# The first x block in two loads, the order of the first products, and fewer warming products, in a float32 kernel of one core

## The chip, the cores and the metric

The kernel runs on 1 core of one Trainium2 chip. The metric is the device time of one execution in microseconds (us); where several executions are shown, their median. A profile comes from one execution, and its own time is given beside it.

## The reference

x is 2048 x 512 (float32). The result mixes two branches with a gate that depends on the row:

```python
g = sigmoid((x * gate_w).sum(-1, keepdims=True))
a = dft_seq_re @ (x @ dft_hid_re.T) - dft_seq_im @ (x @ dft_hid_im.T)   # 2048x2048 and 512x512
b = (silu(x @ w1) * (x @ w3)) @ w2                                      # w1, w3: 512x1376, w2: 1376x512
out = g * a + (1 - g) * b
```

## The kernel before, in words

Products are made in float32 precision out of float32r operands: each operand is split into a rounded part (`high`, a copy on ScalarE, line 108) and the remainder (`low`, a subtraction on VectorE, line 111), and a product of two blocks is three matmuls: rounded x rounded, rounded x remainder, remainder x rounded. Below they are hh, hl and lh, with the weight's part first in the tuple of the code. A block product is done by Strassen's method in Winograd's form (seven products of half blocks instead of eight), so most operands are sums of blocks that VectorE makes.

The kernel writes out its order by hand (`tc.manual_schedule()`, line 427): the order of the calls is the order of each engine's instructions, and each engine and each DMA queue works in that order.

Stages, in order:

1. **The start** (lines 427 to 537). The loads go to SyncE's queue: the first quarter of weight block 0 (`load_w(0, 0, 1)`, 128 x 256), the x block B11 (`load_xo(0, "B11")`, 128 x 1024), the other three quarters of weight block 0, the x blocks B21, B12 and B22, then weight blocks 1 to 3. While they come, TensorE runs `WARM` = 11 products of constants in bfloat16 (lines 432 and 433), whose result nobody reads. The very first column block (weights 0) is not done by Strassen's method but by eight plain half products, `half(i, j, w, x, start)` (line 447): weights' form w (`None` for a21) times x form x (`None` for b12) into the bank C[i, j]. One `half` is six matmuls: two row tiles r of the contraction with hh, hl and lh each. Row tile r reads the x half r (512 columns of the loaded block), so the first row tile needs only the first half of the block. The first call, `half(0, 0, 0, 0, True)` (line 485), reads weights quarter 0 and B11; the second, `half(1, 0, None, 0, True)` (line 487), reads a21 (the fourth quarter of the weights) and B11; the third and fourth (lines 493 and 495) read the second and third quarter and B21; the fifth and sixth (lines 498, 502) read B12.
2. **Gate and up products** (the loop at line 744, `gate_up`), one step for each column block of w1 and w3 and each half of x, with Strassen's seven products.
3. **The spectral branch, the down projection and the hidden DFT** (lines 880 to 1053): `step(m)` for eight blocks of 28 steps or fewer each, one step being 12 matmuls of 512 columns or more. Four blocks of kind F, then two H, then two Y. Six "late" operands (`late_load`, `late_sums` and so on, lines 813 to 844) are loaded, summed, split and stored during the F blocks, hidden beside the products; `late_load` issues its load on SyncE's queue.

The lines that set the order of the first products are these:

```python
hh, lh, hl = (0, 0), (1, 0), (0, 1)
order = [(r, *p) for r in range(2) for p in ((hh, hl, lh) if w is None else (hh, lh, hl))]
if w == x == 0:
    order = [(r, *p) for some in ((hh, lh), (hl,)) for r in range(2) for p in some]
```

`split_by_both` (line 477) rounds a half block with two engines: ScalarE the first 256 columns, VectorE (a copy, line 480) the other 256, and VectorE then makes the remainder.

Of the kernel before, what the change touches and what calls it, by code (L numbers as in the profile page):

```python
# [21 lines left out]
NG = NST // 2  # L22
NC = (F + P - 1) // P
NP2 = (NC + 1) // 2
WARM = 11
LOOK = 3
K = 9
W2_AT = (9, 11, 13, 15)
# [4 lines left out]
def fnet_swiglu_gate_kernel(  # L33
# [20 lines left out]
    nc = tc.nc  # L54
# [25 lines left out]
    def bank(k, name):  # L80
        return psum.tile([P, 512], F32, tag=f"ps{k}", name=name)
# [8 lines left out]
    def take(places, shape, dtype, name):  # L90
        p, tag = at = places.pop(0)
        t = p.tile(shape, dtype, tag=tag, name=name)
        HELD[id(t)] = t, places, at
        return t

    def wide(name):
        return take(F4, [P, 1024], F32, name)
# [9 lines left out]
    def high(hi, src):  # L107
        nc.scalar.activation(hi, src, AF.Copy)  # L108

    def low(hi, lo, src):  # L110
        nc.vector.tensor_sub(lo, src, hi.bitcast(F32))  # L111

    def split(hi, lo, src):
        high(hi, src)
        low(hi, lo, src)
# [5 lines left out]
    def matmul(ps, u, v, some=slice(None), **kw):  # L121
        nc.tensor.matmul(ps.rearrange("p (n a) -> p n a", a=2), u, turns(v)[:, some], **kw)  # L122
# [18 lines left out]
    def flat(ap):  # L141
        return ap.rearrange("p a n -> p (a n)")
# [55 lines left out]
    XO, ST = {}, {}  # L198
    XRAW = ("B12", "B11", "B21", "B22")
# [9 lines left out]
            XO[2] = xo1.tile([P, 2, 2, 512], F32R, tag="xo6", name="xo1_6")  # L209
        return XO[2]  # L210

    def load_xo(g, k):

        if g not in XO:
            XO[g] = (xo1 if g else xo0).tile([P, 2, 7 - g, 2, 512], F32R, tag="xo", name=f"xo{g}")
        ST[g, k] = wide(f"xs{g}_{k}")
        nc.sync.dma_start(ST[g, k], xt[g, XRAW.index(k)])

    OPS = ("B11", "B21", "B22", "T1", "T2", "T3", "T4")
    SUMS = {"T1": ("B12", "B11"), "T2": ("B22", "T1"), "T3": ("B22", "B12"), "T4": ("B21", "T2")}  # L220
# [17 lines left out]
    def load_w(w, lo=0, hi=4):  # L238
        if lo == 0:
            WS[w] = f4_a.tile([P, 4, 256], F32, tag=f"f4_{4 + w % (LOOK + 1)}", name=f"ws{w}")  # L240
        nc.sync.dma_start(WS[w][:, lo:hi].rearrange("p a n -> p (a n)"),  # L241
                          w13[SETS[w], :, lo * 256 : hi * 256])
# [7 lines left out]
    def wa_parts(w, lo, hi):  # L250
        return (*(flat(WA[w][:, h, lo:hi]) for h in range(2)), flat(WS[w][:, lo:hi]))

    def new_wa(w):

        WA[w] = wap.tile([P, 2, 3, 256], F32R, tag="wa", name=f"wa{w}")
# [169 lines left out]


    ctx.enter_context(tc.manual_schedule())
    load_w(0, 0, 1)
    load_xo(0, "B11")
    warm = nc.const_aps.tensor(1.0, [P, 512], mybir.dt.bfloat16)  # L430
    wps = bank(7, "wps")
    for n in range(WARM):
        nc.tensor.matmul(wps, warm[:, :P], warm, start=True, stop=True)
    nc.scalar.activation(act0, warm[:, :24], AF.Silu)
    load_w(0, 1, 4)
    for k in ("B21", "B12", "B22"):
        load_xo(0, k)
    load_w(1)
    load_w(2)
# [7 lines left out]
    def half(i, j, w, x, start):  # L447

        wp = lambda h, sl: a21[:, h, sl] if w is None else WA[0][:, h, w, sl]
        xp = lambda q, h: b12[:, h, q * 512 : (q + 1) * 512] if x is None else XO[0][:, h, x, q, :]
        hh, lh, hl = (0, 0), (1, 0), (0, 1)
        order = [(r, *p) for r in range(2) for p in ((hh, hl, lh) if w is None else (hh, lh, hl))]
        if w == x == 0:
            order = [(r, *p) for some in ((hh, lh), (hl,)) for r in range(2) for p in some]
        for n, (r, u, v) in enumerate(order):
            matmul(C[i, j], wp(u, slice(r * P, (r + 1) * P)), xp(r, v),
                   start=start and n == 0, stop=not start and n == 5)

    def xo_half(k, q):
        i = OPS.index(k)
        return XO[0][:, 0, i, q], XO[0][:, 1, i, q], ST[0, k][:, q * 512 : (q + 1) * 512]
# [8 lines left out]

    t1 = hp.tile([P, 1024], F32, tag="h", name="t1")
    new_wa(0)
    split(*wa_parts(0, 0, 1))

    def split_by_both(hi, lo, src):

        high(hi[:, :256], src[:, :256])
        nc.vector.tensor_copy(hi[:, 256:], src[:, 256:])  # L480
        low(hi, lo, src)

    split_by_both(*xo_half("B11", 0))
    split(*xo_half("B11", 1))
    half(0, 0, 0, 0, True)
    split(a21[:, 0], a21[:, 1], WS[0][:, 3])
    half(1, 0, None, 0, True)
    high(*wa_parts(0, 1, 3)[::2])
    low(*wa_parts(0, 1, 2))
    split_by_both(*xo_half("B21", 0))  # L490
    split(*xo_half("B21", 1))
    low(*wa_parts(0, 2, 3))
    half(0, 0, 1, 1, False)
    split(b12[:, 0], b12[:, 1], ST[0, "B12"])
    half(1, 0, 2, 1, False)
# [63 lines left out]
    for k in ("B11", "B21", "B12", "B22"):  # L559
        do(at_end, 1, load_xo, 1, k)  # L560
# [60 lines left out]
    for n in range(NI):  # L621
        if n in W2_AT:
            p = W2_AT.index(n)
# [4 lines left out]
        if n in A1_AT:  # L628
            p = A1_AT.index(n)
# [183 lines left out]
    def late_load(i, src, tag):  # L813

        r, m = (flat(ut.tile([P, 2, 512], F32, tag=k, name=f"{k}p{i}")) for k in (tag, "c21"))
        nc.sync.dma_start(r, src)
        LATE[i] = [r, m]

    def late_pair(i, j):
# [207 lines left out]
    for i, (src, sp, p) in enumerate(late):  # L1027
        blk, b = 1 + i // 3, i % 3
        n = (10, 17, 24)[b]
        at(blk, n - (5, 5, 6)[b], late_load, i, src[p], ("u3", "u3", "u2")[b])  # L1030
        at(blk, n, late_sums, i)
        at(blk, n + 1, late_split1, i)
        at(blk, n + 2, late_split2, i)
        for j in range(2):
            at(blk, n + 2 + j, late_store, i, j, sp[j][p])
            at(blk, n + 4 + j, late_free, i, j)
# [82 lines left out]
```

## Time and profile before

| | |
|---|---|
| median of 3 runs | 675.94 us (675.76 to 676.01) |
| the profiled execution, its own time | 675.5 us |
| span from its first to its last instruction | 673.7 us |
| mean granted TensorE clock | 1.000 |
| data moved | 172.54 MB, 256 GB/s on average |

The span is the time between the first and the last instruction that the profiler recorded; the chip's own time holds a little more. Engines are PE (TensorE; PEld is its weight loads, which run beside the matmuls), DVE (VectorE), ACT (ScalarE), POOL (GpSimd) and SP (SyncE, which here only issues loads and stores; SPq is its queue). Names such as `xs_B<-xt` are a destination and a source: `xs_B` is a loaded x block, `ws` a loaded weight block, `wa` and `a` split weights, `xo` split x, `C` the banks of the first products, `X`, `Y`, `Z` those of the gate products, `P` those of the last stage. A matmul's recorded length includes the pipeline's end, so its pace is read from the starts.

### The profile page before, as it was taken

To read this page: it belongs to the slowest core of one execution; us is meant where nothing else is said; L and a number is where in the kernel's file an instruction comes from. 1 tells how busy PE (TensorE), PEld (TensorE's weight loads), DVE (VectorE), ACT (ScalarE), POOL (GpSimd) and SP (SyncE) were. 2 spreads that over 40 slices of the span, in tenths; PEclk is the share of its full clock that TensorE was granted. 3 is DMA by queue.
4 is the path that set the end of the run, shared out by engine and by line. 5 is a ranking of instruction groups with operands and counts; after the bars stand their busy time and mean duration, and the time that the engine had idled before them with its cause. 6 is when DMAs were issued, how large, how long until landed. Compare 5 with 4: busy or idle time off the path is not lost.

```text
span 673.7 us, 8669 instructions
## 1 busy us (share of the span) xinstructions
PE 669.4 (99%) x3101; PEld 583.1 (87%) x3101; DVE 601.6 (89%) x748; ACT 371.9 (55%) x496; POOL 64.5 (10%) x119
## 2 busy tenths in 40 slices
PE   9999999999999999999999999999999999999998
PEld 6888888888888888888888888888888888888887
DVE  6999988887779999978999899978896897898996
ACT  6765666655547764465554654554445455455451
POOL 0012112221110000001110101100000000000000
PEclk9999999999999999999999999999999999999999
DMA  7576657599998676715696279919996772874942
GB/s 280 208 293 249 229 200 266 194 357 356 423 418 317 224 216 223 293 63 205 229 386 242 90 252 349 367 57 348 391 341 235 286 259 86 312 277 157 338 134 93
DMA packets 45563, 172.54 MB, mean 256 GB/s; under 512 B 5328, under 2 KB 5712, under 8 KB 41680
## 3 DMA queue, kind: packets, MB, share of 16 engines
q1 hardware_dynamic: 32480, 118.11, 49.0%
q0 software_dynamic: 12752, 53.49, 20.1%
q8 instruction: 24, 0.39, 0.2%
q10 hardware_dynamic: 288, 0.39, 0.2%
q14 instruction: 19, 0.16, 0.1%
HBM read 114.82 MB, written 57.16 MB: 255 GB/s over the span
## 4 chain that ended last, share of the span: by engine, by line
PE 98%; DMA 1%; ACT 0%; DVE 0%; SPq 0%; issue 0%
PE P L122 68%; PE X L122 16%; PE Z L122 8%; PE Y L122 4%; PE C L122 2%; DMA xs_B<-xt 1%; DMA out<-zc 0%; DVE zc L869 0%; ACT xo L108 0%; SPq L241 0%; ACT zc L876 0%
## 5 line engine op out<-in xcount | busy, mean ns | idle before, releaser
L122 PE MATMUL P<-zo,a 128*128 128x512 f32 x1344 | 290.4, 379 | 0.0
L108 ACT ACTIVATE zo<-B 128x1024 fp32r<-128x1024 f32 (+1 forms) x182 | 188.3, 1041 | 176.1 <-PE P L122 79.4
L122 PEld LDWEIGHTS P<-zo,a 128*128 128x128 f32 x1344 | 253.8, 189 | 36.4 <-DVE zo L111 0.4
L111 DVE TENSOR_TENSOR zo<-B,zo 128x1024 fp32r<-128x1024 f32 (+1 forms) x182 | 217.7, 1203 | 29.4 <-ACT zo L108 28.9
L122 PE MATMUL P<-zo,H 128*128 128x512 f32 x468 | 101.2, 379 | 0.0
L122 PEld LDWEIGHTS P<-zo,H 128*128 128x128 f32 x468 | 88.5, 189 | 12.6
L711 DVE TENSOR_TENSOR B<-B,B 128x1024 f32<-128x1024 f32 (+1 forms) x78 | 93.0, 1192 | 0.1
L122 PE MATMUL X<-xo,wb 128*128 128x512 f32 x378 | 88.6, 379 | 0.0
L122 PEld LDWEIGHTS X<-xo,wb 128*128 128x128 f32 x378 | 71.4, 189 | 10.2
L122 PE MATMUL P<-zo,Y 128*128 128x512 f32 (+1 forms) x336 | 71.6, 375 | 0.0
L122 PEld LDWEIGHTS P<-zo,Y 128*128 128x128 f32 x336 | 62.7, 189 | 8.7
L714 DVE TENSOR_TENSOR B<-B,B 128x1024 f32<-128x1024 f32 x26 | 31.7, 1220 | 0.0
L347 POOL DMA_DIRECT2D hsp<-h x40 | 21.7, 544 | 101.4 <-DVE h L407 70.9
L122 PE MATMUL X<-xo,wa 128*128 128x512 f32 x126 | 30.6, 379 | 0.0
L122 PE MATMUL Y<-xo,wa 128*128 128x512 f32 x126 | 30.6, 379 | 0.0
L122 PE MATMUL Z<-xo,wb 128*128 128x512 f32 x126 | 30.6, 379 | 0.0
L122 PE MATMUL Z<-xo,wa 128*128 128x512 f32 x126 | 30.6, 379 | 0.0
L122 PEld LDWEIGHTS X<-xo,wa 128*128 128x128 f32 x126 | 23.8, 189 | 3.4
L122 PEld LDWEIGHTS Y<-xo,wa 128*128 128x128 f32 x126 | 23.8, 189 | 3.4
L122 PEld LDWEIGHTS Z<-xo,wb 128*128 128x128 f32 x126 | 23.8, 189 | 3.4
L122 PEld LDWEIGHTS Z<-xo,wa 128*128 128x128 f32 x126 | 23.8, 189 | 3.4
L967 ACT ACTIVATE zu<-P 128x512 f32<-128x512 f32 x30 | 17.7, 596 | 15.1 <-PE P L122 12.7
(147 smaller groups left out, 552.8 us busy)
## 6 DMA issues: line engine op xcount, KB each, us to landing
B<-cc SPq DMA_DIRECT2D x64, 512.0 KB, 5.8
hsp<-h POOLq DMA_DIRECT2D x40, 256.0 KB, 4.1
B<-hsp SPq DMA_DIRECT2D x20, 512.0 KB, 5.5
wbsp<-wb POOLq DMA_DIRECT2D x8, 1024.0 KB, 4.3
wb<-wbsp SPq DMA_DIRECT2D x8, 1024.0 KB, 7.6
B<-zsp SPq DMA_DIRECT2D x16, 512.0 KB, 8.5
H<-w2sp SPq DMA_DIRECT2D x6, 1024.0 KB, 9.5
ws<-w SPq DMA_DIRECT2D x11, 512.0 KB, 5.0
```

The lines of the kernel that those rows point to most:

```text
L108: nc.scalar.activation(hi, src, AF.Copy)
L111: nc.vector.tensor_sub(lo, src, hi.bitcast(F32))
L122: nc.tensor.matmul(ps.rearrange("p (n a) -> p n a", a=2), u, turns(v)[:, some], **kw)
L347: nc.gpsimd.dma_start(hsp[g, b + k, j // 2, :, j % 2 * 512 : (j % 2 + 1) * 512], h)
L711: nc.vector.tensor_add(t, t, RAW[blk, b, q][:, :n])
L714: nc.vector.tensor_sub(t, RAW[blk, "B12", q], t)
L967: nc.scalar.activation(U[name][:, r], ps[r], AF.Copy)
```

## The change

B11 comes in two loads of 128 x 512, its first half ahead of the first weights' quarter, its second behind it; B21 comes in two loads as well. Eight warming products instead of eleven. B11's first half is rounded by VectorE alone (one copy of 512 columns) and ahead of the weights; its remainder is made before that of the weights. The first `half` goes row tile by row tile: hh, hl, lh for the first, hh, lh, hl for the second. The fifth `half` (weights 0 times b12) does hh and lh of both row tiles and then both hl. The fourth (third quarter times B21) does hl ahead of lh. The third quarter of the weights is rounded behind the first half of B21 instead of together with the second quarter. Of the late loads, those with i = 0 and 3 are issued by GpSimd's queue.

```diff
-WARM = 11
+WARM = 8
...
-    def load_xo(g, k):
+    def load_xo(g, k, some=(0, 2)):
...
-        ST[g, k] = wide(f"xs{g}_{k}")
-        nc.sync.dma_start(ST[g, k], xt[g, XRAW.index(k)])
+        if some[0] == 0:
+            ST[g, k] = wide(f"xs{g}_{k}")
+        b = slice(some[0] * 512, some[1] * 512)
+        nc.sync.dma_start(ST[g, k][:, b], xt[g, XRAW.index(k), :, b])
...
+    load_xo(0, "B11", (0, 1))
     load_w(0, 0, 1)
-    load_xo(0, "B11")
+    load_xo(0, "B11", (1, 2))
...
     load_w(0, 1, 4)
-    for k in ("B21", "B12", "B22"):
+    for q in range(2):
+        load_xo(0, "B21", (q, q + 1))
+    for k in ("B12", "B22"):
         load_xo(0, k)
...
-        order = [(r, *p) for r in range(2) for p in ((hh, hl, lh) if w is None else (hh, lh, hl))]
+        order = [(r, *p) for r in range(2)
+                 for p in ((hh, lh, hl) if w == 1 or w and x == 2 else (hh, hl, lh))]
         if w == x == 0:
+            order[3:] = [(1, *p) for p in (hh, lh, hl)]
+        if w == 0 and x is None:
             order = [(r, *p) for some in ((hh, lh), (hl,)) for r in range(2) for p in some]
...
+    nc.vector.tensor_copy(*xo_half("B11", 0)[::2])
+    low(*xo_half("B11", 0))
     split(*wa_parts(0, 0, 1))
...
-    split_by_both(*xo_half("B11", 0))
     split(*xo_half("B11", 1))
     half(0, 0, 0, 0, True)
     split(a21[:, 0], a21[:, 1], WS[0][:, 3])
     half(1, 0, None, 0, True)
-    high(*wa_parts(0, 1, 3)[::2])
-    low(*wa_parts(0, 1, 2))
+    split(*wa_parts(0, 1, 2))
     split_by_both(*xo_half("B21", 0))
+    high(*wa_parts(0, 2, 3)[::2])
     split(*xo_half("B21", 1))
     low(*wa_parts(0, 2, 3))
     half(0, 0, 1, 1, False)
...
-        nc.sync.dma_start(r, src)
+        (nc.gpsimd if i in (0, 3) else nc.sync).dma_start(r, src)
```

## The prediction

> **What bounds the kernel now.** I read the page's head and its busy shares first, to see whether any engine has idle time to give back.
>
> ```profile
> span 673.7 us, 8669 instructions
> PE 669.4 (99%) x3101; PEld 583.1 (87%) x3101; DVE 601.6 (89%) x748; ACT 371.9 (55%) x496; POOL 64.5 (10%) x119
> ```
>
> TensorE is busy for 99% of the span. The chain that ended last, in order of time, says where the rest lies (start, length, what):
>
> ```profile
> 1.18 3.75 DMA xs_B<-xt
> 5.42 10.88 PE C L122 x48
> ...
> 206.66 461.18 PE P L122 x2136
> 668.58 1.97 DMA out<-zc
> ```
>
> The chain is one load, then TensorE from 5.42 to 668.58 without a break, then the last store. Its main piece runs at 461.18 / 2136 = 0.216 us a product, and that is the full pace: nothing there can be shortened by a load or a split, only by fewer products, and the change keeps the products. So all that this change can win lies ahead of the point from which the products run at 0.216 without a gap. The timeline of the first 17 us finds that point (start, length, engine, line, what, and in brackets the idle time ahead and its releaser).
>
> ```profile
> 0.74 0.39 SPq L241 DMA_DIRECT2D ws<-w  x1
> 0.78 4.33 PE L433 MATMUL wps<-const-bfloat16-1.0 128*128 128x512 bf16 x11 [0.78 <-PEq L1108]
> 1.18 0.42 SPq L217 DMA_DIRECT2D xs_B<-xt  x1
> 1.65 0.42 SPq L241 DMA_DIRECT2D ws<-w  x1
> 2.12 1.48 SPq L217 DMA_DIRECT2D xs_B<-xt  x3
> 3.15 0.42 ACT L108 ACTIVATE wa<-ws 128x256 fp32r<-128x256 f32 x1 [0.89 <-DMA ws<-w]
> 4.96 0.94 ACT L108 ACTIVATE xo<-xs_B 128x256 fp32r<-128x256 f32 x2 [1.39 <-DMA xs_B<-xt]
> 4.96 0.29 DVE L480 CAST xo<-xs_B 128x256 fp32r<-128x256 f32 x1 [0.94 <-DMA xs_B<-xt]
> 5.40 1.29 DVE L111 TENSOR_TENSOR xo<-xs_B,xo 128x512 fp32r<-128x512 f32 x2 [0.15 <-ACT xo L108]
> 5.42 1.81 PE L122 MATMUL C<-xo,wa 128*128 128x512 f32 x6 [0.31 <-ACT xo L108]
> 6.18 0.42 ACT L108 ACTIVATE a<-ws 128x256 fp32r<-128x256 f32 x1 [0.29 <-DMA ws<-w]
> 6.50 0.61 ACT L108 ACTIVATE wa<-ws 128x512 fp32r<-128x512 f32 x1
> 6.63 0.43 DVE L111 TENSOR_TENSOR a<-ws,a 128x256 fp32r<-128x256 f32 x1
> 6.75 0.19 PEld L122 LDWEIGHTS C<-xo,wa 128*128 128x128 f32 x1 [0.29 <-DVE xo L111]
> 7.07 1.46 PE L122 MATMUL C<-xo,a 128*128 128x512 f32 x6
> 7.48 0.94 ACT L108 ACTIVATE xo<-xs_B 128x256 fp32r<-128x256 f32 x2 [0.36 <-DMA xs_B<-xt]
> 8.37 2.75 PE L122 MATMUL C<-xo,wa 128*128 128x512 f32 x12
> 8.72 1.06 ACT L108 ACTIVATE b<-xs_B 128x1024 fp32r<-128x1024 f32 x1 [0.31 <-DMA xs_B<-xt]
> 9.81 1.23 DVE L111 TENSOR_TENSOR b<-xs_B,b 128x1024 fp32r<-128x1024 f32 x1 [0.26 <-ACT b L108]
> 14.61 1.82 DVE L111 TENSOR_TENSOR wa<-ws,wa 128x768 fp32r<-128x768 f32 x2
> 16.14 1.46 PE L122 MATMUL X<-xo,wa 128*128 128x512 f32 x6
> ```
>
> Six products at 0.216 are 1.30 us. The second group, at 7.07, hands over at 8.37, exactly 1.30 later, and the third and fourth (x12) are twice that. The first, at 5.42, takes 1.65. So 0.35 us of gaps lie inside the first group, and the gap-free run begins with the second, at 7.07. Whatever starts earlier must move the third group's start, 8.37, or it moves nothing. The chip's time of this execution is 675.5 us, the span 673.7, so 1.8 us lie around it; the median of the runs shown is 675.94, or 0.44 above this execution. I work in the span and carry the difference over to the median.
>
> **The change part by part: the loads.** One queue carries them. The 131 kB quarter of the weights, issued at 0.74, set ScalarE to work at 3.15; the 524 kB x block behind it did so at 4.96. By then 655 kB had come. In the new order the half block (262 kB) is first, the quarter second, and the other half third, so the 655 kB are complete as before, at 4.96. For the first two I interpolate by bytes between 3.15 and 4.96: half a block at 3.15 + 131/524 x 1.81 = 3.60, the quarter at 4.06. Bounds: not before 3.15, where a load of half the size stood, and not after 4.96.
>
> The weights' other three quarters (393 kB) woke ScalarE at 6.18, the next x block at 7.48, the next at 8.72. That is 1.30 and 1.24 us for 524 kB each. The two extra loads cost SyncE two more issues of some 0.45 us, which put the remaining weights' issue at about 2.1 instead of 1.65, still 4 us ahead of their landing. I take 6.18 and 8.72 as unchanged, and put the first half of B21 at 6.18 + 1.30/2 = 6.83. What each extra load costs beyond its bytes the trace doesn't separate: the bounds are 0 and 0.45 (its issue laid end to end), and I take 0, because the loads already stand back to back in the queue.
>
> The Trainium skill, "DMA: Bandwidth & Descriptors", section "Anatomy of one DMA", gives a fixed 2.0 us per load beside its bytes. Paid one after the other, that would be an estimate of 4 us for the two extra loads, some 679 in all; the wakes 1.30 and 1.24 us apart show that loads in one queue don't pay it one after the other, so it gets no chance below.
>
> **The first group.** Three finer rows give single durations:
>
> ```profile
> 5.28 0.61 ACT L108 ACTIVATE xo<-xs_B 128x512 fp32r<-128x512 f32 x1
> 6.01 0.69 DVE L111 TENSOR_TENSOR xo<-xs_B,xo 128x512 fp32r<-128x512 f32 x1
> 6.75 0.48 PE L122 MATMUL C<-xo,wa 128*128 128x512 f32 x1
> ```
>
> VectorE now copies the whole half. The row has 0.29 for 256 columns; 512 lie between 0.29 and 0.58, and I take 0.42: the 128x256 and 128x512 subtractions (0.43, 0.69) share a fixed part of some 0.16, and 0.29 is that plus 0.13. Copy 3.60 to 4.02, its remainder 4.05 to 4.74, the weights' remainder from 4.66 (two subtractions started 0.61 apart at 5.40 and 6.01) to 5.08. ScalarE rounds the weights from 4.06 to 4.48 (0.42), so the first product is at 4.52, 0.90 earlier. But row tile 1 waits for the second half: rounded by ScalarE 4.96 to 5.57, its remainder 5.60 to 6.29. The new order puts that remainder last, so the sixth product is at 6.33; before, it was at 6.75.
>
> **The second group**, half(1, 0), wants the weights a21. They land at 6.18 as before and are rounded by 6.60, so it starts at 6.64, and this is what ends last. A product that waited takes 0.32 to the next (6.75 to 7.07); the third wants the remainder of a21 (6.64 + 0.43 = 7.07) and waits some 0.03. Six products: 6.64 + 0.32 + 0.22 + 0.25 + 3 x 0.216 = 8.08. **The third group therefore starts at 8.08 instead of 8.37: a gain of 0.29 us**, of the 0.90 by which the first product moved.
>
> **Behind it.** ScalarE rounds wa's second piece from 6.50 to 6.92 (started 0.32 behind a21, as now) and the first 256 columns of B21 by 7.34. VectorE, laid end to end: remainder of a21 to 7.07, of wa's piece to 7.49, the copy of the other 256 columns to 7.78, remainder of B21's first half to 8.50, of its second, 0.61 behind, to 9.11. Group three wants the copy at 8.08, the first remainder with its third product at 8.51 and the second with its sixth at 9.16: it just fits, and each 0.1 us that VectorE is later costs as much. B12 lands at 8.72 and has its remainder at 11.04 (9.81 + 1.23). Group five would start at 10.67; in its old order it would want that remainder at 11.10, in the new one (both remainders last) at 11.53, so that reorder secures the gain and costs nothing. Does VectorE follow?
>
> ```profile
> 8.00:16.00 8.00, 8.00 (x39) 6.93 (x38) 7.68 (x9) 6.35 (x9) 0.00 (x0) 1.00 0.77 313
> 16.00:24.00 8.00, 8.00 (x39) 7.01 (x38) 7.97 (x12) 7.41 (x12) 0.69 (x1) 1.00 0.23 68
> ```
>
> Columns behind the length are busy us of each engine (PE, PEld, DVE, ACT, POOL): VectorE has 7.68 and 7.97 of 8, so it can't move forward by itself. The products have to fit ahead of its results as they stand. The first gate group (16.14, then 15.85) wants the remainder of its weights with its third product, at 16.28; that is done at 14.61 + half of 1.82 = 15.52. The cover is 0.76, above the 0.29.
>
> **The warming products** fall from 11 to 8.
>
> ```profile
> 3.72 0.15 PEld L433 LDWEIGHTS <-const-bfloat16-1.0 128*128 128x128 bf16 x1 [0.28 <-issue]
> 4.14 0.15 PEld L433 LDWEIGHTS <-const-bfloat16-1.0 128*128 128x128 bf16 x1 [0.28 <-issue]
> 4.51 0.10 PEld L433 LDWEIGHTS <-const-bfloat16-1.0 128*128 128x128 bf16 x1 [0.22 <-issue]
> ```
>
> They step by 0.42 to 0.43 and the step shrinks (0.37, and a load of 0.10 for 0.15) between 4.14 and 4.51: TensorE speeds up there. Eight of them stream until about 4.14, so TensorE idles from 4.14 to 4.52. The eleven would have ended at 5.11 and held the first product back by 0.59, but not the second group, which waits for a21; the reduction itself is worth nothing at 8.08. Its price if the speed-up fails to come is the first rival.
>
> **The late loads** with i = 0 and 3 (two of six) move to GpSimd's queue.
>
> ```profile
> 281.26 0.54 POOL L785 DMA_DIRECT2D p5g<-gs  x1 [0.17 <-issue]
> 356.24 0.54 POOL L859 DMA_DIRECT2D zsp<-zc  x1 [2.93 <-DVE zc L857]
> 304.77 0.42 DVE L150 TENSOR_TENSOR c21p<-u3p 128x256 f32<-128x256 f32 x1
> 377.41 0.42 DVE L150 TENSOR_TENSOR c21p<-u3p 128x256 f32<-128x256 f32 x1
> DMA to landing us min/median/max: 4.4/5.8/7.7
> ```
>
> Behind those stores they would be issued at about 281.8 and 356.8 and land within 7.7, at 289.5 and 364.5; the sums that read them start at 304.77 and 377.41. With 13 us of cover I cost them at nothing; behind them on GpSimd wait only stores, which nothing in this stage reads. Without that cover the price would be the delay itself.
>
> **The rivals.** *The speed-up is late* (slower). It came 3.36 to 3.73 us after the first matmul at 0.78. If the idle 0.38 us before 4.52 restarts that count, it comes at 7.9 to 8.25. Until then products step by 0.43: nine have started by 7.96, three more follow at 0.22 or so, and the third group starts near 8.9: 0.5 later than before, 676.4. It decides from the point where the idle stretch is long enough not to count as work. Against it: eight matmuls already fill 3.36 us and the gap is 0.38 long. A second lost period of 3.4 us would add half of it, 1.7: 678.1.
>
> The Trainium skill, "TensorE: Matmul & The Clock Gate", Part 1, says that the full clock follows one busy window of about 3.4 us, in a free-running frame. Eight warming products are just about that long and would seldom fill such a window, which speaks for this rival; the trace's release after 3.36 to 3.73 us agrees with the length, and no trace here shows how much idle a window forgives.
>
> *The gain is lost on the way.* If the smaller loads land 0.3 us later (a21 at 6.48 and B21 behind it; the two unseparated issues would make it at most 0.9), the second group starts at 6.94 and the third near 8.4, or VectorE is that much late for B21's remainders: 675.9. For: each wake hangs on one queue. Against: 1.24 to 1.30 us per 524 kB is steady.
>
> *a21 lands earlier.* Then the second half's remainder (6.33) ends last: 0.31 more at best, 675.3.
>
> **How the numbers follow.** Forecast 0.62: 675.94 - 0.29 = 675.65, rounded to 675.6. Lost on the way 0.17, 675.9. Speed-up late by one period 0.13, 676.4; by two 0.04, 678.1. Earlier a21 0.04, 675.3. The runs shown lie 0.25 apart. The range 675.1 to 676.5 reaches from the last case less that scatter to the first rival and a little beyond. A measurement of this kernel can tell about 0.2%, 1.35 us, from no change, and all cases but the double loss lie within it: same 0.94, slower 0.05, faster 0.01, since 1.35 is more than the first group's gaps and even the whole 0.90 of the earlier first product would give.
>
> **What would show it.** ScalarE's or VectorE's first x work near 3.6 and the first product near 4.5: the loads are right. Second group at 6.6 behind a21, third at 8.1: the sum is right. Products stepping 0.43 beyond 4.6 show the first rival; a21's rounding later than 6.3 shows the second. A gap in TensorE after 9 us, or VectorE waiting for the late loads, would prove me wrong.

## The result, and the profile after

The changed kernel takes 678.0 us (median of 18 runs, 676.25 to 680.41) beside 675.96 for the kernel before (18 runs, 675.68 to 677.98). The ratio is 1.0031, 95% interval 1.0021 to 1.0040: slower by some 2.1 us, and spread over 4.2 us. The profiled execution took 679.74, its span is 678.0.

The chain that ended last in the kernel after (start, length, what), for comparison with 5.42, 206.66 and 461.18 before:

```profile
1.66 5.11 DMA xs_B<-xt
7.47 12.74 PE C L122 x45
...
210.85 461.15 PE P L122 x2136
```

The long stage of products has kept its length, 461.15; it begins 4.19 us later in this execution. So the loss is ahead of it, where the gain was sought. The timeline of the kernel after, its start:

```profile
0.78 3.57 PE L436 MATMUL wps<-const-bfloat16-1.0 128*128 128x512 bf16 x8 [0.78 <-PEq L1117]
4.13 0.43 DVE L483 CAST xo<-xs_B 128x512 fp32r<-128x512 f32 x1 [4.13 <-DMA xs_B<-xt]
4.43 0.42 ACT L108 ACTIVATE wa<-ws 128x256 fp32r<-128x256 f32 x1 [2.18 <-DMA ws<-w]
4.90 1.66 PE L122 MATMUL C<-xo,wa 128*128 128x512 f32 x3 [0.55 <-ACT wa L108]
6.79 0.63 ACT L108 ACTIVATE xo<-xs_B 128x512 fp32r<-128x512 f32 x1 [1.94 <-DMA xs_B<-xt]
7.47 1.65 PE L122 MATMUL C<-xo,wa 128*128 128x512 f32 x3 [0.91 <-ACT xo L108]
7.74 0.42 ACT L108 ACTIVATE a<-ws 128x256 fp32r<-128x256 f32 x1 [0.33 <-DMA ws<-w]
8.91 2.77 PE L122 MATMUL C<-xo,a 128*128 128x512 f32 x6
10.38 1.06 ACT L108 ACTIVATE b<-xs_B 128x1024 fp32r<-128x1024 f32 x1 [0.66 <-DMA xs_B<-xt]
11.47 3.56 PE L122 MATMUL C<-xo,wa 128*128 128x512 f32 x12
14.87 1.46 PE L122 MATMUL C<-b,wa 128*128 128x512 f32 x6
```

Two things are seen. **The data are late**: the second half of B11 is rounded at 6.79 (the whole block: 4.96), a21 at 7.74 (6.18), B12 at 10.38 (8.72), always behind the DMA. **The products are slow**: the second group goes from 8.91 to 11.47, 2.56 us for six where it took 1.30.

The first is plain in the windows' last columns, DMA share and GB/s. Kernel after, then kernel before:

```profile
3.00:4.00 1.00, 1.00 (x4) 0.16 (x2) 0.00 (x0) 0.00 (x0) 0.00 (x0) 1.00 0.75 201
4.00:5.00 1.00, 0.45 (x2) 0.10 (x1) 0.83 (x2) 0.42 (x1) 0.00 (x0) 1.00 1.07 265
5.00:6.00 1.00, 1.00 (x3) 0.76 (x3) 0.62 (x2) 0.00 (x0) 0.00 (x0) 1.00 0.80 221
6.00:7.00 1.00, 0.56 (x2) 0.00 (x0) 0.00 (x0) 0.21 (x1) 0.00 (x0) 1.00 0.79 215
7.00:8.00 1.00, 0.53 (x1) 0.50 (x2) 0.55 (x1) 0.68 (x2) 0.00 (x0) 1.00 1.02 394
```

```profile
3.00:4.00 1.00, 1.00 (x4) 0.31 (x3) 0.41 (x1) 0.42 (x1) 0.00 (x0) 1.00 1.00 375
4.00:5.00 1.00, 1.00 (x4) 0.25 (x2) 0.06 (x2) 0.04 (x1) 0.00 (x0) 1.00 1.01 387
5.00:6.00 1.00, 0.69 (x4) 0.36 (x3) 0.84 (x2) 0.89 (x2) 0.00 (x0) 1.00 1.01 397
6.00:7.00 1.00, 1.00 (x5) 0.68 (x5) 1.00 (x3) 0.82 (x2) 0.00 (x0) 1.00 1.02 410
```

From 3 to 7 us the DMA engines were counted busy for 85% of the time, but moved 0.90 MB (the sum of the four rates) instead of 1.57. The second is plain in the products begun in 2 us, the (x) behind PE's busy time; kernel after, then before:

```profile
8.00:10.00 2.00, 2.00 (x6) 1.53 (x5) 1.85 (x6) 1.72 (x5) 0.00 (x0) 1.00 1.04 424
10.00:12.00 2.00, 2.00 (x6) 1.55 (x6) 1.43 (x3) 1.40 (x2) 0.00 (x0) 1.00 1.02 418
12.00:14.00 2.00, 2.00 (x8) 1.66 (x7) 1.95 (x3) 0.94 (x2) 0.00 (x0) 1.00 1.03 416
14.00:16.00 2.00, 2.00 (x11) 1.75 (x10) 1.97 (x2) 2.00 (x4) 0.00 (x0) 1.00 0.81 324
```

```profile
8.00:10.00 2.00, 2.00 (x11) 1.68 (x10) 1.74 (x4) 1.49 (x3) 0.00 (x0) 1.00 1.04 426
```

"PE busy 2.00" is said of both; only the count tells six from eleven. The full pace comes between 12 and 14 us, and not between 4.14 and 4.51 as before.

My theory from here on: late loads and a late speed-up, and they feed each other, since late data leave TensorE idle. The rivals: the loads alone; the pace alone; the new order of the products; the late loads on GpSimd.

### The profile page after: what moved, and what is told of

Its sections match the earlier page's. It is cut to its first block, busy times and chain, and to the rows that moved or that the text cites. A ratio compares the mean times of both kernels' runs of the same rounds, so it can differ in the third digit from the quotient of the medians.

```text
span 678.0 us, 8669 instructions
## 1 busy us (share of the span) xinstructions
PE 672.4 (99%) x3098; PEld 585.1 (86%) x3098; DVE 601.4 (89%) x748; ACT 371.1 (55%) x496; POOL 65.7 (10%) x121
## 4 chain that ended last, share of the span: by engine, by line
PE 98%; DMA 1%; ACT 0%; SPq 0%; DVE 0%; issue 0%
PE P L122 68%; PE X L122 16%; PE Z L122 8%; PE Y L122 4%; PE C L122 2%; DMA xs_B<-xt 1%; DMA out<-zc 0%; DVE zc L878 0%; ACT xo L108 0%; SPq L243 0%; SPq L219 0%; ACT zc L885 0%
```

## The experiments

Ratios are against the kernel before in the same batch, with 95% intervals.

**e1: the changed kernel, more warming.**

```diff
-WARM = 8
+WARM = 11
```

> The changed kernel with 11 warming products again. Theory Pace (the eight warming products end before the first product, and the idle stretch keeps TensorE at its slow step of 0.43 us): the median comes back to 675.6 to 676.1 and the runs lie within 1 us. Theory Loads (the second half of B11 lands at 6.8 instead of 5.0, and everything behind it follows): still 677 or more, and the profile shows the second half behind 6.5. If both are needed: in between, with a spread of over 2 us.

676.93 (676.17 to 677.28), ratio 1.0015 (1.0006 to 1.0023). The median lies in between, as for two causes, but no expectation is met in full: the spread shrinks from 4.2 to 1.1, and the second half comes at 5.95, not behind 6.5. Its timeline has the full pace at once (six products in 1.29) behind data that are still late:

```profile
5.95 0.63 ACT L108 ACTIVATE xo<-xs_B 128x512 fp32r<-128x512 f32 x1 [1.21 <-DMA xs_B<-xt]
6.96 0.42 ACT L108 ACTIVATE a<-ws 128x256 fp32r<-128x256 f32 x1 [0.39 <-DMA ws<-w]
7.68 1.46 PE L122 MATMUL C<-xo,a 128*128 128x512 f32 x6
8.97 2.75 PE L122 MATMUL C<-xo,wa 128*128 128x512 f32 x12
```

**e2: the kernel before, less warming.**

```diff
-WARM = 11
+WARM = 8
```

> The kernel before with 8 warming products, nothing else changed. Theory Pace: 677 to 679 with a spread of some 3 us, because TensorE idles from 4.14 to 5.42, longer than in the changed kernel. Theory Loads: 675.9 to 676.0 as before.

676.25 (675.62 to 678.01), ratio 1.0010 (1.0001 to 1.0019): the median misses the expectation of Pace, the spread of 2.4 comes near it. Of eleven runs five lie at 675.62 to 675.92, as if nothing had changed, and four at 677.2 to 678.0. So eight warming products are sometimes enough and sometimes not.

**e3 and e5: the changed kernel with the old loads**, with 8 and with 11 warming products.

```diff
-    load_xo(0, "B11", (0, 1))
     load_w(0, 0, 1)
-    load_xo(0, "B11", (1, 2))
+    load_xo(0, "B11")
...
-    for q in range(2):
-        load_xo(0, "B21", (q, q + 1))
-    for k in ("B12", "B22"):
+    for k in ("B21", "B12", "B22"):
```

> The changed kernel with whole loads of B11 (behind the first weights) and B21, so only 8 warming products, the order of the products and the two late loads differ from before. Theory Pace: 677 to 679, wide spread. Theory Loads: 675.7 to 676.1, and narrow.

> The changed kernel with whole loads and 11 warming products: what stays of the change is the order of the products, B11's first half rounded by VectorE alone, and the two late loads on GpSimd. Theory Two Causes (loads that land late, and too little warming, are the whole loss): 675.7 to 676.1. Theory Order (the new order itself costs, since VectorE rounds 512 columns where two engines did 256 each, and the first product starts 0.35 later): 676.2 or more with a first product near 5.75.

e3: 677.79 (677.29 to 678.75), ratio 1.0030 (1.0019 to 1.0041), as Pace expected: without the new loads nearly the whole loss is still there. e5: 676.49 (675.99 to 678.15), ratio 1.0008 (0.9999 to 1.0017). By the ratios three more warming products are worth 1.5 us here; the rest, some 0.5, is what Order said, but its interval reaches no change. e5's first product is at 5.75 as Order expected, where it was at 5.42; of these 0.33 us, 0.22 are B11's, which is rounded at 5.18 in this execution (4.96). The profile of e6 (below), with the old order and B11 rounded at 5.17, is the fairer comparison: its third group begins at 8.65, e5's at 8.98, 0.33 later. The data are nearly back (a21 at 6.41 and 6.26).

**e6: the kernel before with the two late loads on GpSimd.**

```diff
-        nc.sync.dma_start(r, src)
+        (nc.gpsimd if i in (0, 3) else nc.sync).dma_start(r, src)
```

> The kernel before with the late loads 0 and 3 on GpSimd's queue, nothing else. Theory Two Causes: 675.7 to 676.0, no difference, no gap of TensorE behind 275 us that before doesn't have. Theory Late Loads (the moved loads hold up something): 676.2 or more and a gap behind 275 us. Either way it shows whether the 0.3 to 0.9 us gap near 183 us, seen in four kernels and not in two, comes with this edit: if it does, the gap is there again.

676.1 (675.71 to 676.35), ratio 1.0000 (0.9991 to 1.0009). This edit costs nothing. Its profile has a gap of TensorE near 183 us (0.5 us of waiting), as e1's (0.8) and e4's (0.3) have it and not before's. It issues the first moved load only at 282.64, 100 us behind the gap, and up to there it is the kernel before: so the gap can come without any part of the change.

**The loads one by one**, all on the kernel before with 11 warming products. e4 has both splits, e7 B11's alone, e8 both splits with halves that lie dense in memory, e9 both halves of B11 behind the weights, e10 the whole of B11 ahead of them, e11 B21's split alone:

```diff
+    load_xo(0, "B11", (0, 1))        # e4, e7, e8
     load_w(0, 0, 1)
-    load_xo(0, "B11")
+    load_xo(0, "B11", (1, 2))        # e9: (0, 1), then (1, 2); e10: whole, above load_w
...
+    for q in range(2):               # e4, e8, e11
+        load_xo(0, "B21", (q, q + 1))
```

> The kernel before with B11 and B21 each in two loads, the first half of B11 ahead of the weights; 11 warming products and the old order of the products. Theory Pace: 675.6 to 676.1, narrow, since the warming products cover TensorE until 4.95. Theory Loads: 676.5 to 678, the second half of B11 landing behind 6.5.

> The kernel before with B11 alone in two loads, its first half ahead of the weights; B21 whole. If the lateness is paid for each small load at the start: about two thirds to all of the 1.7 us of the kernel with both splits stays (676.8 to 677.4) and a21 is rounded near 7.2. If it came from B21's split: 675.8 to 676.0 and a21 near 6.2.

> The kernel before with B11 and B21 in two loads each, as in the earlier run of that kind, but each half lies without gaps in the device's memory (2 KB rows behind one another and not 4 KB apart). If the 4 KB pitch of half rows is what slows them: 675.7 to 676.2, a21 near 6.2. If the number of loads and rows is what counts: 677.2 to 677.8 again, a21 near 7.4.

> The kernel before with B11 in two loads, both behind the first weights' quarter; B21 whole. Number theory (a further small load among the first ones costs about 1 us whatever its place): a21 is rounded at 6.9 or later, B12 at 9.4 or later, 676.8 to 677.5. Order theory (the loss comes from the x half ahead of the weights): a21 near 6.2, B12 near 8.8, 675.8 to 676.2.

> The kernel before with the whole of B11 ahead of the first weights' quarter: the order changes, the number of loads doesn't. Number theory: a21 near 6.2, B12 near 8.8, 675.7 to 676.2 (the weights wake ScalarE at about 4.9, just behind x). Order theory: a21 at 6.9 or later, 676.8 to 677.5.

> The kernel before with B21 alone in two loads. Both theories: the loads in front are as before, so a21 near 6.2. Number theory taken to every place: B12 some 0.5 later, near 9.2, still ahead of its need, 675.8 to 676.3. If a split costs only while the queue is starting: B12 near 8.8 and 675.8 to 676.0.

The table has the start of the rounding of a21 and of B12 from each timeline, both right behind the DMA or, where ScalarE was busy, behind that:

| kernel | loads on SyncE's queue, kB, in order | a21 | B12 | ratio (interval) |
|---|---|---|---|---|
| before | 131, 524, 393, 524, 524 | 6.18 | 8.72 | |
| e4 | 262, 131, 262, 393, 262, 262, 524 | 7.41 | 9.99 | 1.0027 (1.0017 to 1.0037) |
| e7 | 262, 131, 262, 393, 524, 524 | 7.25 | 9.82 | 1.0023 (1.0012 to 1.0033) |
| e8 | as e4, halves dense | 6.70 | 9.34 | 1.0017 (1.0008 to 1.0026) |
| e9 | 131, 262, 262, 393, 524, 524 | 6.42 | 9.54 | 1.0018 (1.0009 to 1.0027) |
| e10 | 524, 131, 393, 524, 524 | 7.45 | 10.00 | 1.0016 (1.0006 to 1.0027) |
| e11 | 131, 524, 393, 262, 262, 524 | 6.28 | 8.96 | 1.0009 (1.0000 to 1.0019) |

How much these times scatter by themselves is seen in executions whose loads are as before: a21 from 5.87 (e2) to 6.41 (e3), B12 from 8.48 (e2) to 8.97 (e3). So e11's data are not late, and in e9 a21 isn't, but B12 is.

The splits alone, with the old order and all the warming, cost 1.8 us (e4), and nearly all of it is B11's (e7). The pitch of half rows explains at most part: e8 keeps 0.6 of 1.3 us of B12's lateness in its profile (the fastest of its eleven executions), and 1.1 of the 1.8 us by the ratios. Neither number nor order explains it alone: e9 adds a load and keeps the weights ahead, e10 turns the order and adds none, and B12 is late in both. What e4 and e7 to e10 share is a short load (262 kB or less) *behind* another one in the first microseconds. e11, with 677.0 us, lies above both expectations, though its interval reaches no change.

**e13, e15: a piece of the weights on both sides of B11; the weights in one load ahead of it.**

```diff
-    load_w(0, 0, 1)
+    nc.sync.dma_start(WS[0][:, 0, :128], w13[0, :, :128])     # e13
     load_xo(0, "B11")
+    nc.sync.dma_start(WS[0][:, 0, 128:], w13[0, :, 128:256])  # e13
...
+    load_w(0, 0, 4)                                           # e15, ahead of B11
```

> As the kernel before, but the first weights' quarter comes in two pieces of 128 columns, one ahead of the whole of B11 and one behind it. Priming theory (a short first load lets what follows run at full rate): x is rounded near 5.0, a21 near 6.4. Number theory: a21 at 6.9 or later, as with halves behind the weights. Order theory (x ahead of the weights it is used with): a21 near 7.4, as with x first.

> The kernel before with weights block 0 in one load ahead of B11: one load fewer. Number theory: the first 1573 kB (with B21) land earlier than now, B21 rounded at 7.2 or earlier, B12 at 8.4 or earlier; x itself lands later (near 5.9), so that the first product is near 6.3 and the time 676 to 676.4. Otherwise B21 near 7.5 and B12 near 8.7, or later.

e13: 677.86, ratio 1.0026 (1.0017 to 1.0035), a21 at 7.16, B12 at 9.71. A short load in front heals nothing (Priming falls); with a 66 kB load behind B11 the next is 1.0 us late. e15: 676.19, ratio 1.0002 (0.9993 to 1.0012), B21 at 7.40, B12 at 8.69: one load fewer brings nothing; before, those bytes came at 375 to 410 GB/s already (the rows from 3 to 7 us above).

**e14, e16: the first weights, or B11, on ScalarE's queue.**

```diff
-    load_w(0, 0, 1)
+    load_w(0, 0, 1, nc.scalar)         # e14
-    load_xo(0, "B11")
+    load_xo(0, "B11", nc.scalar)       # e16
```

> The kernel before with the first weights' quarter on ScalarE's queue and all else on SyncE's: both queues start at about 0.74. If the start is bound by the order within one queue: x 0.4 earlier, a21 near 5.8, 675.5 to 675.8, the first that beats the kernel before. If concurrent loads of x and weights disturb each other wherever they are queued: a21 at 6.9 or later and 676.8 to 677.5.

> The kernel before with B11 on ScalarE's queue and all else on SyncE's. If only the order within a queue matters: x near 4.9 or earlier and a21 near 6.2 or earlier, since they share the engines, 675.6 to 676. If x and weights disturb each other when they run side by side: x beyond 5.5 and a21 at 6.9 or later, 676.8 to 677.5.

e14: 676.68, ratio 1.0015 (1.0006 to 1.0024); e16: 675.96, ratio 1.0000 (0.9991 to 1.0009). In e14 B11 leads its queue as in e10, but B12 is rounded at 8.44 instead of 10.00; the rate is whole. The two rows of B12, e10 and then e14, and e14's windows from 4 to 7 and from 8 to 9 us:

```profile
10.00 1.06 ACT L108 ACTIVATE b<-xs_B 128x1024 fp32r<-128x1024 f32 x1 [0.33 <-DMA xs_B<-xt]
8.44 1.06 ACT L108 ACTIVATE b<-xs_B 128x1024 fp32r<-128x1024 f32 x1 [0.34 <-DMA xs_B<-xt]
```

```profile
4.00:5.00 1.00, 1.00 (x4) 0.30 (x2) 0.00 (x0) 0.00 (x0) 0.00 (x0) 1.00 0.96 364
5.00:6.00 1.00, 0.63 (x2) 0.00 (x0) 0.49 (x2) 0.94 (x3) 0.00 (x0) 1.00 1.05 428
6.00:7.00 1.00, 0.72 (x2) 0.66 (x3) 0.90 (x3) 1.00 (x3) 0.00 (x0) 1.00 1.01 414
8.00:9.00 1.00, 1.00 (x4) 0.73 (x4) 0.90 (x3) 0.66 (x2) 0.00 (x0) 1.00 1.02 418
```

The loss in time that e14 keeps has another cause: with two queues at work the small weights come at 5.06 only (3.15 before), the first product is at 6.28, and TensorE, which idled for it, then runs at the slow pace (four products begun from 8 to 9, where before had six). So it isn't x beside weights that makes the later blocks late; the short load within SyncE's queue does, or something that goes with it.

**e17: B22, the last block of the burst, in four loads of 131 kB.**

```diff
-    for k in ("B21", "B12", "B22"):
+    for k in ("B21", "B12"):
         load_xo(0, k)
+    for q in range(4):
+        b = slice(q * 256, (q + 1) * 256)
+        nc.sync.dma_start(ST[0, "B22"][:, b], xt[0, XRAW.index("B22"), :, b])
```

> The kernel before with B22, the last of the four x blocks, in four loads of 256 columns (131 kB, 1 KB rows) instead of one. Floor theory: each of the four holds the queue for about 1 us, so that B22's last byte, now at 9.1 us, arrives at 11 to 12.5 and what stands behind it as much later; the first 2097 kB end at 7.9 as before. Starting-phase theory: the four together take the bytes' time and B22 ends at 9.1 to 9.6.

676.38, ratio 1.0005 (0.9996 to 1.0014). The rate falls to 199 GB/s for one microsecond, and B22 is rounded at 10.62 where it was at 9.98: 0.64 for three more loads, some 0.2 each. A floor of 1 us per load falls, and the Starting-phase theory, with 0 to 0.5, is missed by little; four such loads here cost less than the one of e10 (1.28 of B12).

**e18: the changed kernel with B11's first half on ScalarE's queue, B21 whole, 11 warming products.**

```diff
-    load_xo(0, "B11", (0, 1))
+    load_xo(0, "B11", (0, 1), nc.scalar)
```

> The changed kernel with B11's first half on ScalarE's queue, B21 whole, and 11 warming products: SyncE's queue then has one short load in front, the second half of B11, and whole blocks. Floor theory: the first 1048 kB end near 5.4 and B12 at 7.9 as before, first product at 4.4 to 4.8, second group at 6.4 to 6.7, 675.4 to 675.8 and not slower than the kernel before. If a short load slows all queues: 1048 kB at 6 or later and 676.5 to 677.2.

676.05 (675.91 to 676.65), ratio 1.0000 (0.9992 to 1.0009). The lateness is gone as far as the scatter tells (a21 at 6.37, B12 at 8.93; e7, with the same loads in the same order on one queue, 7.25 and 9.82), and the whole loss with it:

```profile
6.37 0.42 ACT L108 ACTIVATE a<-ws 128x256 fp32r<-128x256 f32 x1 [0.34 <-DMA ws<-w]
8.93 1.06 ACT L108 ACTIVATE b<-xs_B 128x1024 fp32r<-128x1024 f32 x1
```

Yet the second half of B11 (262 kB) is still a short load behind another (131 kB) on SyncE's queue. So a short load behind another isn't enough by itself to make the queue late. e18 doesn't beat the kernel before: the weights, beside a second queue, come at 4.55, so the first product is at 5.31. No version measured beats it.

**e12: the changed kernel once more.**

> The changed kernel once more, one look. Theory Pace with a free-running window of some 3.4 us: the speed-up comes at another place than 13.10, anywhere from 3.8 to 14, and the span follows it: about 0.5 us for each us of slow pace. If the place is fixed by the kernel: 13.1 again, within 0.3.

677.39 in this execution, 2.35 less than in the other profile of the same kernel. Its third group begins at 9.83 with products at the full pace:

```profile
4.89 1.25 PE L122 MATMUL C<-xo,wa 128*128 128x512 f32 x3 [0.54 <-ACT wa L108]
6.68 1.21 PE L122 MATMUL C<-xo,wa 128*128 128x512 f32 x3 [0.55 <-ACT xo L108]
8.40 1.59 PE L122 MATMUL C<-xo,a 128*128 128x512 f32 x6 [0.52 <-ACT a L108]
9.83 1.28 PE L122 MATMUL C<-xo,wa 128*128 128x512 f32 x5
```

The place of the speed-up is not the kernel's. With it early, the late data alone put the third group from 8.37 to 9.83, and the fifth from 10.96 to 12.67.

## Why the prediction was wrong

Two steps failed, both put at nothing in the sum that led to 8.08: the two extra loads, and the three warming products that were taken away. Third group: 8.08 forecast, 8.37 before, 11.47 measured.

**The loads: wrong.** I took the first 655 kB "as complete as before, at 4.96" and an extra load at 0 beyond its bytes, with bounds of 0 and 0.45. Measured, the second half came 1.8 us later, a21 1.56 and B12 1.66 (1.3 in e4). How late the second half is differs (6.79 here, 6.00 in e12, 5.95 in e1; in e4 it is rounded by 5.63), but a21 and B12 are late in all five profiles with B11 split ahead of the weights at the old pitch: a21 from 6.96 to 7.94, B12 from 9.80 to 10.92. My rival "the gain is lost on the way" named this mechanism with a chance of 0.17, but at 0.3 us and at most 0.9. My argument for 0 was that the blocks already stood back to back at 1.24 to 1.30 us each. That shows that large loads don't add a cost; it says nothing of short ones, since a short load's own cost, if it runs beside the last one's bytes, can't be seen in 524 kB. The only short load in the trace of before stands first, where nothing is held up.

The 2.0 us per load, to which I gave no chance, come from a section of the Trainium skill ("DMA: Bandwidth & Descriptors", "Anatomy of one DMA") that states them for loads issued by GpSimd; these loads go by SyncE's queue. What e7 and e17 show there, some 1.1 us of B12 for the one more load at the start and 0.2 each for those later on, lies between that figure and my nothing.

**The pace: the right mechanism, with too small a chance and price.** I counted the missing warming products at nothing, and gave the late speed-up 0.13 and 676.4 (0.04 for a second lost period). Twelve of the changed kernel's 18 runs lie above the slowest run of e1 (677.28), so it probably comes in most of them; seen is it in one of two profiles. There it costs more than the loads. Of the fifth group's delay, 3.91 from 10.96 to 14.87, the loads explain 1.71, by e12's 12.67; the pace is the other 2.20 (an estimate, since the loads of the two executions don't land alike). The chain shows it too: from 7.47 to 20.21 TensorE doesn't wait any more, it is only slow at first. I had counted an idle stretch of 0.38; late data made it 0.76 from 4.14 to 4.90, and more before 7.47.

The two don't add up. The new loads alone cost 1.8 us (e4), the eight warming products with the new order alone 2.0 (e3), and all of it together 2.1. So taking the new loads back, with eight warming products, gains nothing in the median (e3), and putting the warming back gains only half (e1, 1.1 us); both must go (e5). The warming is worth 0.7 us on the kernel before (e2) and 1.5 between e3 and e5.

**First product: half right.** 4.90 for 4.52; in this profile each of the first two loads came 0.4 to 0.5 later than the interpolation by bytes (in e1's the half came at 3.48 for 3.60, the weights at 4.32 for 4.06), and the copy took 0.43 as computed (0.42).

**What ends last: half right.** I said a21. In e12 it is a21 (the second group at 8.40, released by a21's rounding). In the profiled kernel after it is the second half of B11, which starts the chain, and then the slow pace:

```profile
1.66 5.11 DMA xs_B<-xt
...
6.79 0.64 ACT xo L108
...
7.47 4.63 PE C L122 x10
```

Right is that an earlier first product moves nothing: e1's is 0.63 earlier than before, its third group 0.60 later.

**The order of the products: right with split loads, probably wrong without.** e1 and e4 both have the new loads and eleven warming products and differ in the order and the rounding (and in the late loads, which cost nothing): every run of e1 (up to 677.28) is faster than every run of e4 (from 677.30). Without the split, in e5, the new order costs up to 0.5. That "the reduction itself is worth nothing" was right as to its gain.

**The late loads: right.** The kernel after issues the first on GpSimd at 286.13 and sums it at 308.95; e6 puts the cost at 0. (The first row I placed it behind, `p5g<-gs`, is itself a load and no store; that changes nothing.)

```profile
286.13 0.55 POOL L825 DMA_DIRECT2D u3p<-w  x1
308.95 0.42 DVE L150 TENSOR_TENSOR c21p<-u3p 128x256 f32<-128x256 f32 x1
```

**A gap behind 9 us:** there is one in the kernel after, 0.27 us near 186, where ScalarE waits for a store (`hsp<-h`) to end. A wait of this kind, of 0.2 to 0.8 us, stands in about half of the twenty profiles, in e6's ahead of anything that its edit moves. So I put it to chance in a stretch of dense transfers; that is argued, not shown. It isn't free in the execution that has it: e1's fifth group is 0.60 later than before's (11.56 for 10.96) and its span 1.4 longer (675.1 for 673.7), and most of the other 0.8 is its wait of 0.8 near 183. One profile's time must be read with this in mind.

**What stays open:** why the queue falls behind when a short load follows another one in the first microseconds. In e4, e7 to e10 and e13 it does; where a short load is moved to ScalarE's queue it doesn't (e10 to e14, e7 to e18), though e18 keeps a short load behind another. Later in the burst the cost shrinks (e17, e11), and the half rows' pitch has at most a part. Open is also why one of the kernel before's 18 runs took 677.98 with all eleven warming products; it has no profile.

## What to carry to other kernels

Splitting the first load to start sooner is only worth it if what ends last comes sooner too; here the second group waited for a later load, and that one became late. Price a short load among the first ones by a run of its own, since here one load more made all behind it over 1 us late; a second queue cured that, but brought the first weights later. Read the GB/s of each microsecond, not the DMA share. Warm TensorE up to the first real product with no idle stretch, and judge such a change by many runs: the span of one profile of the changed kernel said +4.3 us, another's +1.9. And undo the parts one by one and together: here undoing either of two alone gave no more than half.

## What the runs showed of the hardware

**The clock is taken away and given back in a window of some 3.4 us.** In e10 TensorE idled over 2 us before its first product at 7.08, and the granted clock (the column behind POOL's) shows the pace taken away and given back:

```profile
6.00:7.00 1.00, 0.00 (x0) 0.00 (x0) 0.63 (x2) 1.00 (x3) 0.00 (x0) 1.00 0.99 382
7.00:8.00 1.00, 0.92 (x3) 0.78 (x4) 0.96 (x2) 0.65 (x3) 0.00 (x0) 0.64 0.99 389
8.00:9.00 1.00, 1.00 (x4) 0.82 (x3) 1.00 (x4) 0.65 (x2) 0.00 (x0) 0.50 1.03 422
9.00:10.00 1.00, 1.00 (x3) 0.74 (x3) 0.90 (x4) 0.67 (x3) 0.00 (x0) 0.50 1.03 422
10.00:11.00 1.00, 1.00 (x5) 0.84 (x3) 0.94 (x3) 1.00 (x1) 0.00 (x0) 0.65 1.00 410
```

A share of 0.64 is half pace for 0.72 us, from 7.28; 0.65 is half pace for 0.70, to 10.70: 3.42 us. The Trainium skill, "TensorE: Matmul & The Clock Gate", Part 1, gives a free-running window of 3413 ns, and a kernel whose warming differs from run to run; these rows agree with the length, and the two profiles of the changed kernel with the difference from run to run. Four of the changed kernel's 18 runs, of 677.98 to 679.27 us, show the same mean clock of 0.997 as e10's profiled one; 1.71 us of lost clock (half of 3.42) are 0.25% of the span. The granted clock doesn't show the slow pace before the first release: it reads 1.00 in the kernel after from 8 to 12, where the products count six in 2 us.

**A short load on another queue.** The Trainium skill, "DMA: Bandwidth & Descriptors", section "Issuing engines are not separate DMA queues", has it that a second issuing engine saves only the time of the issue. Here the measurement differs: an issue takes 0.42, and moving the 131 kB load from behind B11 to ScalarE's queue (e10 to e14) brought B12 forward by 1.56.
